# A hybrid attention layer with a written-out instruction order: two loads for two blocks, other engines for the first statistics, other heads in the memory products, and another order

## The chip, the core and the metric

The program runs on one core of a Trainium2 chip. Five engines work side by side, each through its own instructions in order: TensorE (PE; its weight loads are PEld), VectorE (DVE), ScalarE (ACT), GpSimd (POOL) and SyncE (SP), which here only issues transfers. They wait for each other through semaphores. Matrix products land in PSUM, which this kernel uses as 8 banks of 128 x 512 floats. The metric is the device time of one execution in microseconds; lower is better.

## What is computed

The input x has 2048 tokens of width 640. Two residual blocks follow each other:

```
h  = x + A(layernorm(x))           # attention with a memory, 32 heads of 20
h2 = h + silu(layernorm(h) @ w1) @ w2     # 640 -> 1728 -> 640
```

A cuts the tokens into four segments of 512. In each segment and head it forms

```
a_dot = softmax(q k^T * scale + causal mask) v
a_mem = phi(q) M / (phi(q) z + 1e-6)       # phi(t) = t + 1 if t > 0 else exp(t)
o     = g * a_mem + (1 - g) * a_dot        # g = sigmoid(beta), one per head
M    += phi(k)^T v ;  z += sum phi(k)      # for the segments that follow
```

and the four segments' o go through wo. Segment 0 has an empty memory.

## The kernel before

**Layout.** Tokens are handled in 16 blocks of 128, four to a segment. The 32 heads are packed for the array in groups of 128 rows: four heads to a group, 32 rows to a head, of which 20 are used. Heads 0 to 19 fill five groups; the 12 spare rows below the heads of the first three groups, and those of the last two, hold the dimensions of heads 20 to 31, which three further groups (QKV) get by small copies (`vt`). So a segment has eight groups, called ticks here and numbered 0 to 31 over the four segments.

**Tasks.** The work is cut into named tasks, each of which emits the instructions of one step on one engine. The names that the text uses, s a segment, b a block, k a tick:

- `x0, x1, x2, x4, x8, x12`: loads of x. `w_*`: loads of weights. `re_wq0..4`, `re_wk0..4`: copies that rearrange the columns of wq and wk into the packed layout; chunk 0 comes in two halves (`re_wq0`, `re_wq0h`). They can run on ACT, DVE or POOL.
- `n1_st`, `n1_rs`, `n1_ap`, `n1_tp`, `n1_te`, `n1_tr` (b): first layer norm of a block: statistics; one over the root, on POOL; normalization, on DVE; transposes, on PE with an evacuation `te` for blocks 0 to 3, by DMA (`tr`) for the others. `n2_*` is the second layer norm.
- `pr` (segment, group, 0 for q and 1 for k): projections; `qe` evacuates them from PSUM. `ex`, `pa`, `pb`: phi, an exp on ACT and two steps on DVE. `v`, `ve`: the same for v.
- `qk k a|b|e`: scores of a tick, on PE, into four banks; `e k a|b|e`: their exp on ACT, in two instructions of 128 x 1024, or in one of 128 x 2048 where the list says `/W`; `mk`: causal masks on POOL; `av`: products with v; `oe`: their evacuation; `td`, `tm`: transposes back and products with the memory; `nm`: division, on DVE; `ad`: the sum of both parts, on POOL. The e scores serve two ticks.
- `kt`, `mz`, `ma`, `mb`: update of the memory. `ot`, `wo`, `rs`: output projection and first residual. `h1`, `th`, `s`: first matrix of the second block, and silu by a tanh on ACT and a step on DVE. `h2`, `o`, `out`: second matrix, second residual and store.

**Order.** No planner runs when the kernel is built: the whole order of 1432 entries is written out as one list, `ORDER`. Each entry names a task, the engine if there is a choice (`/A` ACT, `/D` DVE, `/G` POOL, `/C` column-tiled products on PE, four 32-column products in place of one), and the buffers it takes (`qk4a0:4,6` takes the PSUM banks 4, 5 and 6, 7). `schedule` replays it, and each engine's program is the list restricted to that engine. A tracker sets the semaphore waits. So an engine never overtakes: an entry that waits holds up all that follow it on its engine, and a bank is given to a new task only behind the task that empties it.

**PE's modes.** PE's products come in three forms: whole array (projections, h1, h2), 32-column tiles (`av`, `mz`, `/C` entries) and 32-row tiles (`qk`). `fill25` and `fill5` are products with zeros ahead of the first real work.

The layer norm's tasks are made in `layer_norm` (L734 on), the memory update in `declare_memory` (L1092 on), the loads in `build` (L584 on).

## Time and profile before

| | |
|---|---|
| median of 3 runs | 296.02 us (295.38 to 296.52) |
| the profiled execution | 295.39 us |
| its span, first to last instruction | 293.7 us |
| TensorE clock granted, mean | 0.999 |
| busy share: PE, DVE, ACT, POOL | 97%, 74%, 74%, 50% |
| instructions: PE, DVE, ACT, POOL | 3786, 450, 258, 294 |

Around the span lie 1.7 us of the time. Instruction durations in the groups include the pipeline's depth, so neighbours on an engine overlap by some 0.1 us; where instructions follow each other without a gap, the time of the merged row divided by their number is the better cost of one. Line numbers (L965) are those of the kernel before.

### The profile page before, as it was taken

Reading aid. Unit: us, or ns where it says so; the run is one execution under the profiler, and the core shown is the slowest. Engines: PE = TensorE matmul, PEld = TensorE weight load, DVE = VectorE, ACT = ScalarE, POOL = GpSimd, SP = SyncE. Lnnn points to the kernel's source line nnn. Section 1 sums busy time; section 2 is a strip of 40 time slices with the busy share of each in tenths; the row PEclk is TensorE's granted clock in tenths of the full one; section 3 lists DMA queues with packets and bytes.
Section 4 is the critical chain, followed back from the end, with each engine's and each line's share of the span. In section 5 each row is a group of like instructions: output and inputs, shape, how many; then the busy total and the mean of one; then the engine's idle time right before and its main releaser. Section 6 shows DMA issues by size and latency. Waiting matters only on the chain.

```text
span 293.7 us, 8932 instructions
## 1 busy us (share of the span) xinstructions
PE 284.1 (97%) x3786; PEld 158.3 (54%) x3786; DVE 217.8 (74%) x450; ACT 216.8 (74%) x258; POOL 147.9 (50%) x294
## 2 busy tenths in 40 slices
...
GB/s 218 336 74 189 144 47 215 122 77 69 113 133 85 141 2 2 148 106 63 92 73 82 46 78 69 35 2 42 90 21 2 2 37 122 77 104 0 0 2 112
DMA packets 48599, 24.75 MB, mean 84 GB/s; under 512 B 38896, under 2 KB 47472, under 8 KB 48560
## 3 DMA queue, kind: packets, MB, share of 16 engines
...
q14 instruction: 9, 0.07, 0.1%
...
## 4 chain that ended last, share of the span: by engine, by line
PE 83%; ACT 8%; DVE 4%; POOL 2%; issue 1%; DMA 1%; ACTq 0%; DVEq 0%
PE ps_all L551 56%; PE ps_all L552 13%; PE ps_all L944 7%; ACT PT L965 6%; PE ps_all L1000 5%; ACT PT L961 1%; POOL rst L767 1%; PE ps_all L1118 1%; DVE stt L755 1%; PE ps_all L1204 1%; DMA x_tok<-in_A_x_dram 1%; DVE xn_rot L773 1%; POOL PT L977 0%; DVE oTs L1016 0%; POOL rst L765 0%
## 5 line engine op out<-in xcount | busy, mean ns | idle before, releaser
L977 POOL TENSOR_SCALAR_AFFINE_SELECT PT<-PT 128x512 bf16<-128x512 bf16 x128 | 83.1, 656 | 51.4 <-ACT PT L965 33.3
L965 ACT ACTIVATE PT<-ps_all 128x1024 bf16<-128x1024 f32 x100 | 96.5, 1038 | 9.2 <-PE ps_all L944 7.5
L961 ACT ACTIVATE PT<-ps_all 128x2048 bf16<-128x2048 f32 x30 | 56.4, 1880 | 7.9 <-PE ps_all L944 7.3
L551 PE MATMUL ps_all<-w_sb,sT 128*128 128x320 bf16 x420 | 61.1, 299 | 0.2
L1217 ACT ACTIVATE th<-ps_all 128x512 f32<-128x512 f32 (+1 forms) x56 | 31.6, 585 | 36.3 <-PE ps_all L551 29.6
L1223 DVE SCALAR_TENSOR_TENSOR sT<-th,ps_all 128x512 bf16<-128x512 f32 (+1 forms) x56 | 36.0, 662 | 24.5 <-ACT th L1217 24.4
L551 PE MATMUL ps_all<-tT,w_sb 128*128 128x512 bf16 x211 | 50.7, 380 | 0.0
L551 PEld LDWEIGHTS ps_all<-w_sb,sT 128*128 128x128 bf16 x420 | 40.1, 98 | 18.0 <-issue 1.6
L551 PEld LDWEIGHTS ps_all<-tT,w_sb 128*128 128x128 bf16 x211 | 19.1, 98 | 22.1 <-issue 1.6
L1078 POOL TENSOR_TENSOR otok<-on 128x320 bf16<-128x320 bf16 x24 | 19.2, 800 | 18.6 <-DVE on L1070 14.6
L755 DVE BATCH_NORM_STATS2 stt<-x_tok 128x6 f32<-128x320 bf16 x60 | 26.2, 479 | 2.3 <-DMA x_tok<-in_A_x_dram 2.0
L1260 DVE SCALAR_TENSOR_TENSOR x_tok<-ps_all,x_tok 128x640 bf16<-128x640 f32 (+1 forms) x17 | 13.2, 782 | 17.3 <-PE ps_all L551 16.6
L765 POOL TENSOR_TENSOR rst<-mvt,eps_c 128x1 f32<-128x1 f32 x32 | 6.6, 206 | 32.1 <-DVE mvt L758 32.0
L868 DVE CAST QK<-ps_all 128x512 bf16<-128x512 f32 x25 | 17.1, 685 | 5.8 <-PE ps_all L551 3.4
L1070 DVE TENSOR_TENSOR on<-ps_all,rd 128x640 bf16<-128x640 f32 x24 | 19.8, 824 | 0.8
L1016 DVE TENSOR_SCALAR oTs<-ps_all,lsc 128x512 bf16<-128x512 f32 x25 | 18.4, 741 | 1.4 <-PE ps_all L1000 1.4
L767 POOL TENSOR_TENSOR rst<-rst,eps_c 128x1 f32<-128x1 f32 x32 | 18.1, 566 | 2.5
L773 DVE TENSOR_SCALAR xn_rot<-x_tok,mvt,rst 128x640 bf16<-128x640 bf16 x32 | 16.5, 519 | 3.6 <-POOL rst L767 2.3
L551 PE MATMUL ps_all<-tT,wkr 128*128 128x512 bf16 (+1 forms) x76 | 18.8, 372 | 0.1
L551 PE MATMUL ps_all<-tT,wqr 128*128 128x512 bf16 (+1 forms) x72 | 18.2, 369 | 0.2
L1000 PE MATMUL ps_all<-PT,Vx 128*32 128x512 bf16 (+3 forms) x384 | 17.0, 301 | 0.1
L551 PE MATMUL ps_all<-wv_sb,tT 128*128 128x320 bf16 x100 | 15.6, 299 | 0.5 <-ACT PT L965 0.4
...
## 6 DMA issues: line engine op xcount, KB each, us to landing
...
x_tok<-in_A_x_dram SPq DMA_DIRECT2D x3, 640.0 KB, 4.6
...
w_sb<-in_B_w_dram SPq DMA_DIRECT2D x1, 640.0 KB, 4.6
```

Source lines behind the costliest of these rows:

```text
L551: return [lambda e: e.matmul(out, lhsT=lhsT, rhs=rhs, start=start, stop=stop)]
L552: return [lambda e, p=p: e.matmul(out[p:p + 32, :], lhsT=lhsT[:, p:p + 32], rhs=rhs, start=start, stop=stop, tile_position=(0, p)) for p i ...
L755: T.add(DV, lambda e, hh=hh: e.bn_stats(out=stt[:, s, 6 * hh:6 * hh + 6], in_=xb[:, 320 * hh:320 * hh + 320]), reads=R((xa, xsub)), writes ...
L767: T.add(PO, lambda e: e.tensor_tensor(out=rst[:, s, :], in0=rst[:, s, :], in1=eps_c[:, 1:2], op=ALU.pow), reads=R((st, ["r"]), (C, ["half" ...
L944: fns.append(lambda e, j=j, o=o, r=r, q0=q0, q1=q1, qa=qa, ka=ka: e.matmul(ps_all[:, o:o + q1 - q0], lhsT=ka[32 * r:32 * r + DH, 128 * j:1 ...
L961: T.add(AC, lambda e: e.activation(out=o, in_=src, func=ACT.Exp, scale=SCALE), reads=[("ps", z.slot + q) for z in (a, b) for q in range(2) ...
L965: T.add(AC, lambda e: e.activation(out=pt[:, pta.slot, q0:q0 + 2, 0:width], in_=sc3[:, b0:b0 + 2, 0:width], func=ACT.Exp, scale=SCALE), re ...
L977: fns.append(lambda e, v=v: e.affine_select(out=v, in_=v, pattern=[[0, 4], [1, 128]], compare_op=ALU.is_ge, fill=0.0, base=0, channel_mult ...
L1000: fns.append(lambda e, j=j, r=r, h=h, pa=pa, pt=pt, co=co, q0=q0, ji=ji: e.matmul(bank(po)[32 * r:32 * r + 32, q0:hi], lhsT=vtile(vx)[:, j ...
L1070: T.add(DV, lambda e: e.tensor_tensor(out=on[:, ona.slot, :, :].rearrange("p b (x e) -> p b x e", e=DH), in0=v[:, :, :, 0:DH], in1=r2.unsq ...
L1217: T.add(AC, lambda e: e.activation(out=th[:, tha.slot, lo:hi], in_=bank(ps)[:, lo:hi], func=ACT.Tanh, scale=0.5), reads=R((ps, [0])), writ ...
L1223: T.add(DV, lambda e: e.scalar_tensor_tensor(out=sT[:, f, lo:hi], in0=th[:, tha.slot, lo:hi], scalar=1.0, in1=bank(ps)[:, lo:hi], op0=ALU. ...
```

## The change

Five things change together.

1. Blocks 2 and 3 of x come by two loads of 160 KB, not by one of 320 KB.
2. Statistics of blocks 0, 1 and 3 are made on DVE, that of block 2 on ACT; before, blocks 1 and 2 were on ACT. On ACT the mean is now scaled in its own instruction (`n1_mn2`), off the way to the variance.
3. For blocks 0, 1 and 3 the small constant under the root is added on DVE at the end of the statistics, so that POOL makes the root with one instruction (pow) in place of two (add, pow).
4. In the memory update the second head of the first three groups is 20 heads on, not 16: the layout puts head 20 + 4c + r below head 4c + r. The products keep their number and size; with stride 16 the rows of phi(k) of one head met the values of another.
5. `ORDER` is another list of 1433 entries. Nearly every entry changes place, and some change engine: on POOL there are 8 `re` entries in place of 5, on ACT 12 `oe` in place of 7, 6 `ve` in place of 9, and 31 exps `/W` in place of 30. PE has the same 510 tasks in both lists.

The code that changes:

```diff
-    load_x(2, 2, -97, 4.79, "fix", (SP,))
+    load_x(2, 1, -97, 2.4, "fix", (SP,))
+    load_x(3, 1, -96.5, 2.4, "fix", (SP,))
...
-                T.add(AC, lambda e: e.activation(out=o, in_=xb, func=ACT.Identity, scale=1.0 / D, accum_out=mvt[:, s, 0:1]),
-                      reads=R((xa, xsub)), writes=R((st, ["mv"]), (xn, [0])))
-                T.add(AC, lambda e: e.activation(out=stt[:, s, 0:1], in_=mvt[:, s, 0:1], func=ACT.Identity, scale=f),
-                      reads=R((st, ["mv"])), writes=R((st, ["s0", "s1"])))
+                T.add(AC, lambda e: e.activation(out=o, in_=xb, func=ACT.Identity, scale=f / D, accum_out=stt[:, s, 0:1]),
+                      reads=R((xa, xsub)), writes=R((st, ["s0"]), (xn, [0])))
...
+            if early:
+                T.add(DV, lambda e: e.tensor_scalar(out=mvt[:, s, 1:2], in0=mvt[:, s, 1:2], scalar1=EPS, scalar2=None,
+                                                    op0=ALU.add),
+                      reads=R((st, ["mv"])), writes=R((st, ["mv"])))
+        early = tag == "n1_" and b in (0, 1, 3)
+        onact = tag == "n1_" and b == 2
...
+            if early:
+                T.add(PO, lambda e: e.tensor_tensor(out=rst[:, s, :], in0=mvt[:, s, 1:2], in1=eps_c[:, 1:2], op=ALU.pow),
+                      reads=R((st, ["mv"]), (C, ["half"])), writes=R((st, ["r"])))
+                return
...
-                heads = [(4 * c, 16, 2)] if c < 3 else [(12, 8, 3)] if c == 3 else [(16, 8, 2), (28, 1, 1)]
+                heads = [(4 * c, 20, 2)] if c < 3 else [(12, 8, 3)] if c == 3 else [(16, 8, 2), (28, 1, 1)]
```

The start of the list, up to the scores of tick 2, before and after:

```diff
-epsg0:0 halfc epsc zpad warm:0 iota x0:1 n1_st0:3 x1:0 x2:2,3 w_q0:0 w_q1 w_k0 w_k1 w_wv:0 beta sel n1_st1/A:0,3
-fill25:3 n1_rs0 n1_ap0:0 n1_tp0:3 mt3 mta3 fill5:0 n1_st2/A:4,2 n1_st3:1 n1_rs1 n1_ap1 n1_tp1:0 n1_te0/D:1 re_wq0/A:0
-mt0 n1_rs3 n1_ap3:3 n1_tp3:6 n1_te1 n1_rs2 mt2 re_wq0h/G n1_ap2 n1_te3 re_wk0:0 re_wq1/G x4:4,5,6,11 n1_tp2:4 n1_te2
-pr000x.0:0 pr000x.1 qe000x/D:0 re_wk0h re_wq2 pr001x.0:7 pr001y.0:3 pr000y.0:1 pr000y.1/C qe000y/D x8:8,7,10,9
-pr001y.1/C qe001y/D pr001x.1/C qe001x ex001:0 pr010.0/C:4 qk0a0:2,6 e0a2:6 pr010.1 qe010/D:0 re_wk1/G re_wq3 pr011.0:1
-pr011.1 qe011/D zf0 zf1 e0a0 qk0b0:4,6 e0b2/W:5 lsc0 mtb3 re_wk4/G re_wk2 re_wq4 mta0 mtb0 mta2 mtb2 mm10 mzc10 mm9
-mm11 re_wk3/G pa001:2 pb001 pr020.0:0 pr020.1 qe020:0 pr021.0:1 pr021.1 qk0e0:2,4 v01.0/C:6 n1_st4:5 mm8 n1_rs4 vpad2
-mk0a e0e2/W:3 qe021/D vt06:0 n1_st7:1 mk0b n1_rs7 vt03 w_w1_1:0 vt09 n1_ap4:2 n1_tr4:0 kt00:0 vt00 n1_st11:5 w_w1_4
-ex021:0 v00.0/C:0 v00.1 ve00:0 qk1a0:2,4 e1a2:0 e1a0 v01.1/C ve01/D mk1a n1_st6:2 n1_rs6 v02.0/C:0 v02.1/C ve02
-n1_st5:6 n1_rs5 qk1b0:4,6 e1b0/W:4 pr031.0:3 pr031.1 qe031/D:0 ex031:1 n1_ap6:0 v03.0:0 v03.1 ve03 qk2a0:2,6 e2a0:1
...
+mt3:0 mt2 x0:4 x1:8 x2:9 x3:0 zpad warm:0 mt1 iota sel mta2 mt0 vpad0 fill25:2 fill5:0 n1_st2:2,3 n1_mn2 n1_st0:4
+halfc w_q0:0 n1_st1:7 w_q1 w_k0 w_k1 w_wv:0 n1_rs0 mta3 n1_ap0:2 n1_tp0:0 n1_te0:1 n1_st3:0 n1_rs1 n1_ap1:0 n1_tp1:2
+epsc n1_rs2 n1_ap2 n1_tp2:4 n1_rs3 n1_ap3:2 n1_tp3:6 re_wq0/G:0 re_wq1/G mta0 mtb0 n1_te1 pr000x.0/C:3 re_wq0h
+pr000x.1 n1_te2/D n1_te3 qe000x:0 pr000y.0:5 pr000y.1 qe000y re_wk0:0 pr001y.0:0 pr001x.0:7 x4:1,2,10,3 re_wk0h
+pr001y.1 re_wq2/A pr001x.1 qe001x qe001y/D ex001:1 pr010.0:1 qk0a0:4,6 e0a0:6 pr010.1 qe010/D:0 e0a2 pr020.0:2 pr020.1
+qk0b0:4,0 e0b0:3 e0b2 beta w_wo:0 qe020/D:0 pa001:0 pb001 mm4 vpad1 mtb2 re_wk1/G pr011.0/C:3 pr011.1/C epsg0 qe011/D
+ex011:0 re_wk3/G mtb3 mm10 re_wk2/G pr021.0/C:7 pr021.1/C re_wq3/G re_wk4/G vpad2 mm11 mta1 qk0e0:2,4 e0e0/W:2 v00.0:0
+lsc0 v00.1 ve00:0 n1_st4:7 mm2 n1_rs4 re_wq4/G mm0 n1_st7:5 n1_rs7 mk0b qe021/D v01.0:6 kt00:0 w_w1_3:0 n1_ap4:3
+n1_st6:0 vt00:0 n1_tr4:2 x8:5,6,7,11 lsc1 qk1a0:4,2 e1a0/W:0 ex021:1 v01.1 ve01/D mtb1 mm1 v02.0:0 v02.1/C n1_st5:1
+n1_rs5 qk1b0:4,6 ve02/D n1_ap7:0 pr031.0:2 pr031.1 qe031/D:0 zf0 e1b0/W:4 v03.0:0 v03.1 ve03/D pa031:1 n1_rs6 n1_ap6:2
+mm8 ex031:2 pb031 n1_st10:2 qk2a0:3,6 e2a0:1 pr030.0/C:2 pr030.1 n1_ap5:3 lsc2 qe030/D zf1 mm3 mk0a mm6 mk1a e2a2
```

Around the scores of tick 23, before and after:

```diff
-ad19 n1_rs13 h1_1_7_0.1/C th1_7_0:0 s1_7_0 h1_1_8_0.1/C th1_8_0:1 av21:3 oe21:0 h1_1_9_0.0:4 h1_1_9_0.1 th1_9_0:0
-h1_1_10_0.0:7 n1_ap14:2 s1_8_0 v30.0:5 v30.1 ve30:1 s1_9_0 n1_ap13:1 tm21:2 h1_1_10_0.1 td21 th1_10_0:1 nm21:0,1
-qk23a0:5,0 e23a2:2 mk22e s1_10_0 n1_ap15:3 h1_1_11_0.0:4 h1_1_11_0.1 e23a0 mk22a qk23b0:0,2 e23b2/W:1 th1_11_0:1 ad21
...
+th1_4_0:0 s1_4_0 qk22e0:2,4 th1_8_0:1 s1_8_0 mk21b av21:0 e22e2/W:1 h1_1_9_0.0:6 n1_st13:3 n1_st15:2 ad19 n1_rs14
+n1_ap14:2 n1_tr14 n1_rs13 n1_rs15 th1_6_0:1 h1_1_7_0.0:7 h1_1_7_0.1 th1_7_0:0 s1_7_0 n1_ap13:3 n1_tr13 s1_6_0 oe21:1
+h1_1_9_0.1 th1_9_0:0 s1_9_0 tm21/C:2 v30.0/C:4 v30.1/C ve30:0 mk22a h1_1_10_0.0/C:7 h1_1_10_0.1/C th1_10_0:1
+qk23a0:4,0 e23a2:5 mk22b mk22e e23a0 mk23a td21 nm21:1,0 h1_1_11_0.0:6 h1_1_11_0.1 n1_ap15:0 n1_tr15 kt21:4 s1_10_0
+qk23b0:0,2 e23b0/W:3 th1_11_0:1 v32.0/C:4 v32.1/C ve32/D av22:7 oe22/D:0 ex241:0 v31.0/C:0 v31.1/C ve31 mk23b ad21
```

185 lines of the change are left out of this document (94 added, 91 removed).

## The prediction

> **What bounds the kernel now.** I read the page's busy shares first, then the table of stretches, then what PE waited for.
>
> ```profile
> PE 284.1 (97%) x3786; PEld 158.3 (54%) x3786; DVE 217.8 (74%) x450; ACT 216.8 (74%) x258; POOL 147.9 (50%) x294
> ```
>
> PE is busy for 284.1 of 293.7 us, but a busy PE need not be at its peak. The stretches say where it is idle; the first numbers behind the length are the busy times of PE, PEld, DVE, ACT and POOL.
>
> ```profile
> 0.00:10.00 10.00, 7.61 (x53) 5.48 (x54) 5.40 (x15) 8.26 (x17) 5.59 (x24) 1.00 0.81 261
> 10.00:30.00 20.00, 19.98 (x263) 9.96 (x265) 17.67 (x51) 18.03 (x22) 15.81 (x42) 1.00 0.73 177
> 30.00:40.00 10.00, 8.13 (x181) 4.13 (x169) 8.75 (x20) 9.68 (x12) 8.04 (x18) 1.00 0.43 98
> 40.00:50.00 10.00, 8.73 (x137) 3.85 (x138) 8.36 (x20) 9.87 (x13) 7.92 (x20) 1.00 0.60 170
> 50.00:60.00 10.00, 9.75 (x151) 4.39 (x148) 8.33 (x18) 9.86 (x12) 5.84 (x12) 1.00 0.50 105
> 60.00:270.00 210.00, 208.82 (x2883) 117.08 (x2876) 159.59 (x317) 156.30 (x180) 104.66 (x179) 1.00 0.36 67
> ```
>
> So there are three places to gain or lose. Up to 10 us PE has little real work. From 30 to 60 it idles 1.87 + 1.27 + 0.25 = 3.39 us, while ACT is busy 29.41 of 30: this stage runs at ACT's pace. From 60 on it idles 1.18 us in 210. The rest is PE's own work.
>
> **PE's work does not change.** Counted in the two lists, PE has the same 510 tasks with the same columns, and in both 188 of them follow a task of another array form. More entries are column-tiled in some places and fewer in others; the tiles' four products run side by side. The other heads (stride 20 for 16) leave the memory products' count and sizes alone. I take 0 for all of this. The last entries, `h2_13_3_0` to `out13_1`, are the same, so the end behind 291 us stays.
>
> **The front.** The rows of the first ten microseconds (start, length):
>
> ```profile
> 0.80 1.36 SPq L584 DMA_DIRECT2D x_tok<-in_A_x_dram  x3
> 3.09 0.89 DVE L755 BATCH_NORM_STATS2 stt<-x_tok 128x6 f32<-128x320 bf16 x2 [2.02 <-DMA x_tok<-in_A_x_dram]
> 4.01 0.21 DVE L758 BATCH_NORM_AGGREGATE mvt<-stt 128x2 f32<-128x12 f32 x1
> 4.30 0.19 POOL L765 TENSOR_TENSOR rst<-mvt,eps_c 128x1 f32<-128x1 f32 x1 [3.04 <-DVE mvt L758]
> 4.57 0.56 POOL L767 TENSOR_TENSOR rst<-rst,eps_c 128x1 f32<-128x1 f32 x1
> 5.25 0.54 DVE L773 TENSOR_SCALAR xn_rot<-x_tok,mvt,rst 128x640 bf16<-128x640 bf16 x1 [0.94 <-POOL mt L670]
> 7.08 0.82 DVE L792 CAST tT<-ps_all 128x640 bf16<-128x640 f32 x1
> 8.89 0.45 DVE L773 TENSOR_SCALAR xn_rot<-x_tok,mvt,rst 128x640 bf16<-128x640 bf16 x1 [0.51 <-POOL rst L767]
> 9.40 0.45 PE L782 MATMUL ps_all<-ident,xn_rot 128*128 128x128 bf16 x5 [0.51 <-DVE xn_rot L773]
> 9.46 0.85 DVE L714 COPY wkr<-sT 128x240 bf16<-128x240 bf16 x2
> 9.69 0.71 PE L551 MATMUL ps_all<-tT,wqr 128*128 128x256 bf16 x5
> 10.47 0.85 POOL L714 COPY wkr<-sT 128x400 bf16<-128x400 bf16 x2 [0.21 <-DMA sT<-in_A_wk_dram]
> x_tok<-in_A_x_dram SPq DMA_DIRECT2D x3, 640.0 KB, 4.6
> L662 DVE TENSOR_SCALAR zf<-zf 128x32 f32<-128x32 f32 x1 | 0.2, 173 | 0.0
> L657 DVE TENSOR_SCALAR lsc<-lsc 128x8 f32<-128x8 f32 x1 | 0.7, 674 | 0.0
> ```
>
> Now DVE makes three statistics, each 0.89 + 0.21 and the added constant. No row shows that addition; the small ones give 0.17 to 0.67, and I take 0.2, as most small ones are near the lower end. Statistics of block 0 then end at 4.45. The new list puts those of block 1 ahead of the first normalization on DVE: 4.45 + 1.3 = 5.75, and the saved POOL step (0.19 + 0.08) is lost there, since the root is ready at 5.06. Normalization 0 ends at 6.25 (before: 5.79), statistics 3 at 7.55, and normalizations 1, 2, 3 at 0.45 each at 8.9, against 9.34 before. Block 2 is not on this path as long as its statistics on ACT and its two POOL steps (0.19 + 0.56) end before 8.0, when normalization 2 comes up; x2 is issued where the pair was, with half the bytes. So the last transposes end near 9.4 and not 9.85, and the first projection can start at 9.4, not 9.69.
>
> Part of this is given back. DVE then has, in a row, two copies of chunk 0 of wq (some 0.6), an evacuation of 0.82 and the two copies of wk's chunk 0 (0.85): the last end near 11.2, some 0.2 after PE has made the query products that stand before the key products. The extra load pushes the weights' issues by one, 1.36/3 = 0.45; the keys' second part, awaited on POOL until 10.47, is now due near 10.9, before DVE reaches it. `x4` waits for those copies of wk, so it leaves SP near 11.2; it takes 4.6 and is there at 15.8, before its statistics, which stand behind the products of v at some 18 us. The load of wo moves up to the place right behind it on SP, where nothing early follows but transposes of block 4. Sum: -0.2, between -0.6 (all of the earlier start stays) and +0.8 (the addition at 0.67 three times, less the 0.6).
>
> **The stage at ACT's pace.**
>
> ```profile
> 20.17 0.71 ACT L833 ACTIVATE sT<-ps_all 128x640 bf16<-128x640 f32 x1
> 25.52 0.33 PE ps_all L944 x4
> 25.13 0.63 ACT L874 ACTIVATE ex<-w_sb 128x512 bf16<-128x512 bf16 x1
> 26.25 1.93 ACT L965 ACTIVATE PT<-ps_all 128x1024 bf16<-128x1024 f32 x2
> 28.06 1.89 ACT L961 ACTIVATE PT<-ps_all 128x2048 bf16<-128x2048 f32 x1
> 30.79 18.68 ACT L965 ACTIVATE PT<-ps_all 128x1024 bf16<-128x1024 f32 x20 [0.32 <-PE ps_all L944]
> L1014 ACT ACTIVATE oTs<-ps_all,lsc 128x512 bf16<-128x512 f32 x7 | 4.7, 686 | 0.9 <-PE ps_all L1000 0.9
> ```
>
> In a run one half exp costs 18.68/20 = 0.93, so two cost what one `/W` costs (1.89 less its overlap): merging gains nothing. From the first exp of tick 0 to the last of tick 7 the old list has 32 halves, 4 whole ones, 4 `ex`, 3 `ve`, 1 `qe`; the new one 30, 5, 5, 1, 1 and one `oe`. That is +0.63 - 2 x 0.70 + 0.69 = -0.1. Moreover two `ve` and a `qe` of those saved, less an `ex`, lie before the scores of tick 2, where PE and not ACT sets the pace (PE idles 0.02 of 20 us): the new ACT stands idle there, and all it gains is its backlog: the scores of tick 2 are ready at 25.52 + 0.33, and ACT came to them at 26.25, 0.4 later. One idle time of 0.32 at 30.79 may go or stay. Net -0.1 from the list and -0.2, half of the backlog: -0.3. Ends: -1.2 and +0.9. The gain would be PE work drawn into the idle time: ahead of the scores of tick 9 the new list has all memory products and one half projection (3 x 0.24) more, and one of 2 x 0.24 less. The loss would be `oe1` at 0.69 right before the exps of tick 4, whose scores wait for it in turn, and 0.2 of a new idle time.
>
> ```profile
> 183.43 0.93 PE ps_all L1118 x94
> L551 PE MATMUL ps_all<-tT,w_sb 128*128 128x512 bf16 x211 | 50.7, 380 | 0.0
> ```
>
> 0.93 + 0.72 - 0.48 = 1.2 us: the lower end. I take less because at the scores of tick 10 both lists have called the same PE work but for one half of `wo1`, which the new one lacks.
>
> **The one long wait behind 60 us.**
>
> ```profile
> 164.94 0.55 POOL L767 TENSOR_TENSOR rst<-rst,eps_c 128x1 f32<-128x1 f32 x1
> 165.52 0.74 DVE L773 TENSOR_SCALAR xn_rot<-x_tok,mvt,rst 128x640 bf16<-128x640 bf16 x1 [0.27 <-POOL rst L767]
> 166.19 0.18 DVE L1064 TENSOR_TENSOR rd<-ps_all,epsg 128x32 f32<-128x32 f32 x1
> 166.78 0.82 DVE L1070 TENSOR_TENSOR on<-ps_all,rd 128x640 bf16<-128x640 f32 x1
> 167.75 0.40 PE L944 MATMUL ps_all<-QKV 20*128 20x384 bf16 x8 [0.66 <-DVE on L1070]
> ```
>
> Scores 23b need the bank of `nm21`; on DVE `nm21` stands behind `n1_ap13`, which waits for a root that POOL makes only behind masks and an `ad`. In the new list root and normalization come well ahead, but `nm21` itself (166.19 to 167.60, 1.4) now starts when `td21` ends and is covered by four to five products of 0.24 alone, 1.2. What is late next is `nm21`, by some 0.3. I take -0.3, between -0.66 and +0.5 (a bank that comes free later by another step of 0.8). Other waits of the new order can't be read in a trace of the old one: between 0 and +1.2, what 210 us now hold; I take 0, since both lists leave the same 188 changes of form and as much PE work between the scores.
>
> Sum: -0.2 - 0.3 - 0.3 = -0.8. The profiled execution took 295.39, so 294.6; the median of the runs stands 0.63 above it, so 295.2.
>
> **Rivals.**
>
> *Faster by over 0.5%* (what a measurement of this kernel can tell from no change; 1.48 us). The work drawn forward fills PE's idle time: -1.2 there, -0.6 in the front, -0.66 at tick 23: 296.02 - 2.5 = 293.6. For it: PE idle is 3.39 us and the list does call more PE work by tick 9. Against it: scores wait for banks that ACT empties, and ACT's list is as long as before.
>
> *Slower by over 0.5%.* POOL comes too late in the front. It gets `re_wq0`, `re_wk2`, `re_wq3` and `re_wq4` and loses `re_wq0h`.
>
> ```profile
> L714 POOL COPY wkr<-sT 128x400 bf16<-128x400 bf16 x3 | 1.5, 515 | 0.2 <-DMA sT<-in_A_wk_dram 0.2
> L714 POOL COPY wkr<-sT 128x240 bf16<-128x240 bf16 x1 | 0.4, 388 | 0.0
> L881 DVE TENSOR_SCALAR phiK<-w_sb 128x512 bf16<-128x512 bf16 x1 | 0.6, 622 | 0.0
> L881 DVE TENSOR_SCALAR phiQ<-QK 128x512 bf16<-128x512 bf16 x15 | 6.4, 429 | 0.0
> ```
>
> Chunk 2 is 0.52 + 0.39, and the last two chunks have two small copies for the second: 1.2 each; in sum 3.4 us more. POOL idles 4.2 us between 10 and 30, so by the sum it fits, with 0.8 to spare. But `pr021` waits for `re_wk2`: from the last early root near 8.2 POOL has chunks wq0, wq1, wk1, wk3 and some eight constants of 0.2 to 0.3 before it, which makes 15; PE needs it after 29 products of 0.24 or less from 9.4 on, at 16.3 or sooner. From some 1.3 us late on, PE idles as long as POOL is late, exps start late, and nothing behind gives it back; past 2.3 us of it the kernel is over 0.5% slower. All 3.4 us exposed give 295.2 + 3.4 = 298.6.
>
> *DVE slows beside POOL's copies.* A `pa` step beside a copy of POOL took 622 ns, the others 429 on average: 0.19. The new list has 20 such copies for 12; 8 x 0.19 = 1.5 us on DVE, which is busy 17.67 of 20 there. All of it exposed gives 296.7, within 0.5%. The Trainium skill ("SBUF — State Buffer", the single rule on the shared port pair) has it that VectorE and GpSimd hold that pair exclusively for a whole instruction, the other waiting; the two rows here agree in direction, with 0.19 us. By that rule alone each of the eight could hold DVE for a copy's whole length; as an estimate that is 8 x 0.4 = 3.2 us and 298.4.
>
> *The front is not earlier.* Statistics 1 stand ahead of normalization 0, so the first transposes come no sooner, and the additions cost 0.4 each: the front's +0.8, 296.2.
>
> **How the numbers follow.** The forecast 0.33; faster 0.32; DVE beside copies 0.07 and no earlier front 0.07, both within 0.5%; slower 0.21, most of it POOL, some a new wait that I did not see. That gives 0.32, 0.47, 0.21. The forecast's own range is 293.9 (-0.6 - 1.2 - 0.3 = -2.1) to 296.4 (+1.2, the new waits' end). The full range, 292.7 to 297.8, takes in the faster case and slower ones up to 2.6 us of exposed delay.
>
> **What would show it.** Right: the first projection at 9.2 to 9.6 us; PE idle of 2.3 to 3.6 us between 30 and 60 with ACT at 9.6 of 10 or more; no PE wait of over 0.4 us near 165. Wrong: PE idle between 10 and 30 above 0.5 us, which would be POOL or DVE in the front; ACT idle over 1 us in 30 to 60; PE idle behind 60 above 2 us; or PE's busy time itself other than 284.

## The result, and the profile after

Over six executions the changed kernel takes 298.80 us in the median (298.25 to 301.83); the kernel before, beside it, 295.83 (295.13 to 296.52). The ratio is 1.0119, with a 95% interval of 1.0073 to 1.0166. A repetition (told below) gives 298.86 against 295.56, 1.0092 [1.0065, 1.0118]. So the change costs some 3 us, about 1%. The forecast was 295.2, with a range up to 297.8: wrong in sign, and the time lies above the range. The profiled execution took 298.25, its span 296.3, which is 2.6 more than before.

The table of stretches of the changed kernel, with the columns as in the prediction (length; busy PE, PEld, DVE, ACT, POOL; clock; then the DMA engines' share and GB/s):

```profile
0.00:10.00 10.00, 7.43 (x64) 5.16 (x64) 7.32 (x21) 6.51 (x10) 6.41 (x25) 1.00 0.79 246
10.00:30.00 20.00, 19.41 (x195) 9.34 (x193) 16.33 (x37) 18.15 (x23) 16.84 (x52) 1.00 0.84 212
30.00:40.00 10.00, 7.20 (x147) 3.64 (x146) 8.76 (x23) 8.93 (x10) 7.45 (x15) 1.00 0.43 91
40.00:50.00 10.00, 8.52 (x128) 3.14 (x124) 7.25 (x16) 9.89 (x12) 7.26 (x16) 1.00 0.46 104
50.00:60.00 10.00, 9.41 (x181) 4.88 (x177) 9.37 (x21) 9.89 (x12) 6.33 (x14) 1.00 0.62 148
60.00:270.00 210.00, 208.11 (x3055) 116.89 (x3040) 157.19 (x315) 157.59 (x181) 105.38 (x181) 1.00 0.34 66
```

The reader is to see three things. PE idles 0.59 us between 10 and 30 (before 0.02), 4.87 between 30 and 60 (before 3.39) and 1.89 from 60 to 270 (before 1.18). ACT, which should set the pace from 30 on, has 1.07 us idle between 30 and 40 alone, where it had 0.32. And PE's busy time over the whole span is 283.8 against 284.1: its work is the same, so all of the loss is idle time. The waits of PE in the changed kernel (engine, buffer and line; what it waited for; us in total, times, the longest):

```profile
PE ps_all L959 <- ACT PT L976: 1.4, 2, 0.8
PE ps_all L797 <- DVE xn_rot L788: 1.3, 2, 1.1
PE ps_all L959 <- ACT PT L980: 1.2, 4, 0.5
...
PE ps_all L1015 <- DVE w_sb L883: 0.9, 1, 0.9
PE ps_all L551 <- DVE Vx L849: 0.6, 1, 0.6
PE ps_all L959 <- DVE otok L1067: 0.6, 1, 0.6
...
PE ps_all L551 <- DVE tT L807: 0.3, 1, 0.3
...
PE ps_all L551 <- DVE wqr L715: 0.2, 1, 0.2
```

The waits for `PT` are scores that want banks which exps still empty. Those of 0.9 for `w_sb` and of 0.6 for `otok` (a division on DVE, which holds up scores of tick 5) were not there before, and no step of the prediction has them.

Following the same tasks of PE through both traces shows where the 2.7 us arise. Start in the changed kernel less start in the one before:

| task | us |
|---|---|
| first projection `pr000x` | -0.6 |
| scores of tick 0, 1, 2 | +0.1, +0.3, +0.3 |
| scores of tick 3 | +1.4 |
| scores of tick 4 and 7 | +2.0, +2.1 |
| scores of tick 10 (less PE's own work done by then) | +1.6 |
| scores of tick 12 (the same) | +2.3 |
| scores of tick 24, 31, end | +3.0, +2.7, +2.7 |

In the two corrected rows PE's idle time is compared in place of its starts; they are good to some 0.2. So in this execution the front loses 0.3, the stage between 25 and 51 us about 1.8, some 0.5 comes back by tick 10, and 0.7 goes near 82 us. Behind that little more is lost.

**The front.** Rows of the timeline of the changed kernel:

```profile
4.26 0.15 DVE L760 TENSOR_SCALAR mvt<-mvt 128x1 f32<-128x1 f32 x1
4.66 0.74 ACT L747 ACTIVATE xn_rot<-x_tok 128x640 bf16<-128x640 bf16 x1 [1.32 <-DMA x_tok<-in_A_x_dram]
9.05 0.63 DVE L715 COPY wqr<-sT 128x160 bf16<-128x160 bf16 x2 [0.43 <-DMA sT<-in_A_wq_dram]
9.06 0.51 PE L552 MATMUL ps_all<-tT,wqr 128*32 128x256 bf16 x12
...
15.60 1.01 DVE L896 TENSOR_SCALAR phiK<-w_sb 128x512 bf16<-128x512 bf16 x1
```

The added constant costs 0.15, not 0.2, and the first projection starts at 9.06, 0.6 earlier. But its second half waits for weights that land later than before, as the prediction said of the issue order, and an evacuation comes behind the copies of those weights on DVE: 0.2 and 0.3 us in the table of waits. By the first scores nothing is left. By those of tick 1 it is +0.3: the step at 15.60 takes 1.01 beside copies on POOL (the same line takes 0.28 alone, see the run with the masks moved), and the next scores wait 0.26 for the evacuation behind it. The front isn't the same in every execution, though. The repetition of this kernel has +0.3 at tick 2 again. But in seven other profiles of kernels with the same list up to here, or with a few masks moved in it, the scores of tick 2 stand at -0.4 to -0.1, and in three where block 2 lands late at +1.0 to +1.2. So a loss in the front is not shown.

**The stage at ACT's pace.** The timeline from 24 to 32 us, DVE, then POOL, ACT and PE:

```profile
26.60 0.75 DVE L896 TENSOR_SCALAR phiK<-w_sb 128x512 bf16<-128x512 bf16 x1
27.27 0.75 DVE L788 TENSOR_SCALAR xn_rot<-x_tok,mvt,rst 128x640 bf16<-128x640 bf16 x1
27.94 0.88 DVE L902 TENSOR_TENSOR phiK<-phiK,ex 128x512 bf16<-128x512 bf16 x1
28.75 0.89 DVE L754 BATCH_NORM_STATS2 stt<-x_tok 128x6 f32<-128x320 bf16 x2
...
30.20 0.68 DVE L883 CAST w_sb<-ps_all 128x512 bf16<-128x512 f32 x1
...
30.95 0.68 DVE L883 CAST w_sb<-ps_all 128x512 bf16<-128x512 f32 x1
...
26.56 1.98 POOL L992 TENSOR_SCALAR_AFFINE_SELECT PT<-PT 128x512 bf16<-128x512 bf16 x3
...
31.67 0.63 ACT L889 ACTIVATE ex<-w_sb 128x512 bf16<-128x512 bf16 x1 [0.99 <-DVE w_sb L883]
...
37.58 0.72 ACT L1029 ACTIVATE oTs<-ps_all,lsc 128x512 bf16<-128x512 f32 x1
...
28.80 1.24 PE L551 MATMUL ps_all<-tT,wqr 128*128 128x512 bf16 x5
30.93 0.73 PE L1015 MATMUL ps_all<-PT,sT 128*32 128x512 bf16 x16 [0.89 <-DVE w_sb L883]
```

DVE is late here, and both PE and ACT wait for it. PE's `av0` needs the bank that `qe030` empties (the cast at 30.20): 0.89. ACT's `ex041` needs what `qe041` writes (the cast at 30.95): 0.99, in a stage in which ACT's time is the stage's time. On DVE the statistics of block 10 (28.75) stand ahead of both, and ahead of those three steps lie that take 0.75, 0.75 and 0.88 beside POOL's masks. The load of blocks 8 to 11 (`x8`) lands at 28.72 in this trace, so the statistics could not have started sooner in any case. At 37.58 stands `oe1` on ACT, right before the exps of tick 4, as the prediction said it would.

**Near 82 us and near 170 us.**

```profile
79.63 1.46 DVE L788 TENSOR_SCALAR xn_rot<-x_tok,mvt,rst 128x640 bf16<-128x640 bf16 x2
81.02 0.85 DVE L902 TENSOR_TENSOR phiQ<-phiQ,ex 128x512 bf16<-128x512 bf16 x1
81.79 0.81 DVE L849 CAST Vx<-ps_all 128x640 bf16<-128x640 f32 x1
82.66 0.32 PE L551 MATMUL ps_all<-Mzb,phiQ 128*128 128x84 bf16 x4 [0.56 <-DVE Vx L849]
168.65 0.19 DVE L1079 TENSOR_TENSOR rd<-ps_all,epsg 128x32 f32<-128x32 f32 x1 [0.81 <-PE ps_all L551]
...
169.26 0.82 DVE L1085 TENSOR_TENSOR on<-ps_all,rd 128x640 bf16<-128x640 f32 x1
168.44 1.25 PE L551 MATMUL ps_all<-tT,w_sb 128*128 128x512 bf16 x5
170.23 0.40 PE L959 MATMUL ps_all<-QKV 20*128 20x384 bf16 x8 [0.54 <-DVE on L1085]
```

`tm8` takes the bank that `ve23` empties, and `ve23` stands on DVE behind a queue without gaps whose steps are long again. The wait at tick 23, which was to go, is still there: 0.54 in place of 0.66.

### The profile page after: what moved, and what is told of

The parts are those of the page before. It is cut to its first block, busy times and chain, and to the rows that moved or that the text cites. A ratio compares the mean times of both kernels' runs of the same rounds, so it can differ in the third digit from the quotient of the medians.

```text
span 296.3 us, 9115 instructions
## 1 busy us (share of the span) xinstructions
PE 283.8 (96%) x3873; PEld 157.6 (53%) x3873; DVE 216.5 (73%) x445; ACT 216.9 (73%) x255; POOL 149.7 (51%) x299
## 4 chain that ended last, share of the span: by engine, by line
PE 76%; DVE 11%; ACT 8%; DMA 2%; issue 1%; SPq 1%; DVEq 0%; ACTq 0%
PE ps_all L551 52%; PE ps_all L552 11%; PE ps_all L959 7%; ACT PT L980 6%; PE ps_all L1015 4%; DMA sT<-in_A_wq_dram 2%; DVE xn_rot L788 2%; ACT PT L976 1%; DVE phiQ L902 1%; DVE stt L754 1%; PE ps_all L1133 1%; DVE oTs L1031 1%; DVE on L1085 1%; PE ps_all L1219 1%; DVE x_tok L1197 1%
## 5 line engine op out<-in xcount | busy, mean ns | idle before, releaser
L980 ACT ACTIVATE PT<-ps_all 128x1024 bf16<-128x1024 f32 x98 | 94.3, 1025 | 12.3 <-PE ps_all L959 10.7
L976 ACT ACTIVATE PT<-ps_all 128x2048 bf16<-128x2048 f32 x31 | 58.3, 1880 | 3.8 <-PE ps_all L959 3.3
L551 PE MATMUL ps_all<-w_sb,sT 128*128 128x320 bf16 x374 | 53.8, 299 | 0.0
L551 PE MATMUL ps_all<-tT,w_sb 128*128 128x512 bf16 x202 | 46.9, 379 | 0.0
L551 PEld LDWEIGHTS ps_all<-w_sb,sT 128*128 128x128 bf16 x374 | 35.6, 98 | 15.3 <-issue 1.5
L551 PE MATMUL ps_all<-tT,wqr 128*128 128x512 bf16 (+1 forms) x82 | 20.3, 371 | 0.7 <-DVE tT L807 0.3
L780 POOL TENSOR_TENSOR rst<-mvt,eps_c 128x1 f32<-128x1 f32 x29 | 6.2, 215 | 27.2 <-DVE mvt L757 27.1
L551 PE MATMUL ps_all<-wo_sb,tT 128*128 128x320 bf16 x120 | 17.9, 299 | 0.0
L782 POOL TENSOR_TENSOR rst<-rst,eps_c 128x1 f32<-128x1 f32 x29 | 16.4, 567 | 2.3
L1031 DVE TENSOR_SCALAR oTs<-ps_all,lsc 128x512 bf16<-128x512 f32 x20 | 14.8, 745 | 3.4 <-PE ps_all L1015 3.3
L551 PE MATMUL ps_all<-wv_sb,tT 128*128 128x320 bf16 x110 | 17.0, 299 | 0.4 <-ACT PT L980 0.2
```

Source lines behind the costliest of these rows:

```text
L551: return [lambda e: e.matmul(out, lhsT=lhsT, rhs=rhs, start=start, stop=stop)]
L976: T.add(AC, lambda e: e.activation(out=o, in_=src, func=ACT.Exp, scale=SCALE), reads=[("ps", z.slot + q) for z in (a, b) for q in range(2) ...
L980: T.add(AC, lambda e: e.activation(out=pt[:, pta.slot, q0:q0 + 2, 0:width], in_=sc3[:, b0:b0 + 2, 0:width], func=ACT.Exp, scale=SCALE), re ...
```

## The experiments

All ratios are to the kernel before, run beside. The kernel before and the two built on its code (the old list with the new one behind it, and the old list with `nm21` moved) keep its head stride of 16 in the memory update; all others have 20. "The end" is the start of PE's last product in the profiled execution less that of the kernel before (the changed kernel: +2.7); these come from one execution each, so the ratio stands beside them. A part of each end is the front, which varies, so the shift of PE's scores is also given from tick 2 to tick 7, which is the stage alone:

| kernel | at tick 2 | from tick 2 to 7 | from 7 to the end |
|---|---|---|---|
| changed | +0.3 | +1.8 | +0.5 |
| the same, repeated | +0.3 | +1.7 | +0.5 |
| DVE's order | -0.2 | +1.1 | +0.8 |
| with `oe1` on DVE too | -0.1 | +0.8 | +0.3 |
| all mends | +1.1 | +0.8 | +0.2 |

The expectations name theories by letters; those on which the readings rest are: A, DVE is late near 30 us, and `oe1` on ACT costs its length; F and M, the bank layout of the scores of ticks 3 and 4; G, POOL's masks lengthen DVE's steps; J, the late load `x8`; N, the granted clock.

### The code alone

The four edits of the code (loads, statistics, root, heads) with the list of before:

```diff
-x2:2,3
+x2:2 x3:3
-n1_st1/A:0,3
+n1_st1:0
-n1_st2/A:4,2
+n1_st2:4,2 n1_mn2
-n1_ap1
+n1_ap1:1
```

> The old list with all four changes of the code (x2 and x3 in two loads, statistics of block 3 on VectorE, the constant added on VectorE and one GpSimd step per root, stride 20 in the memory products) and none of the new order. Theory A (the loss of the changed kernel comes from the new order; its pieces: 1.1 us where DVE reaches two evacuations late near 30 us, 0.6 us for oe1 on ACT near 38 us, 0.7 us of a wait near 83 us): the parts cost nothing that lasts, ratio to the kernel before 0.997 to 1.003. Rival B (the added DVE steps and the extra load cost, and the order only shows it): 1.004 or more, with the shift in place before the scores of tick 1.

Measured: 295.97, 1.0026 [0.9998, 1.0054]. The four parts cost nothing that can be told from no change, so the new list holds most of the loss. In this trace the first scores come 0.6 later and the end 0.4; the old front itself comes out 0.1 and 0.4 later in two other kernels that have it unchanged.

### Half of the list

One kernel has the old list up to the scores of tick 9 and the new one behind; the other the new one up to the exps of tick 9 and the old one behind.

> The kernel before, its list up to the scores qk9a0 (near 60 us), then what is left in the order of the new list (with some other buffers, 14 of them). In the traces PE's start times less its own work stand 1.9 us later in the changed kernel at that place and 2.7 us at the end. Theory A: the first 1.9 is absent and 0.8 stays, most of it the wait at 83 us: +0.8 us, ratio 1.003. Rival C (what is lost early is regained by other idle time, and the loss is made behind 60 us): +2.7 us, ratio 1.009.

Measured: 313.39, 1.0604 [1.057, 1.0639]. This settles nothing: the joint itself broke the order. Wait table of this kernel:

```profile
PE ps_all L552 <- DVE QK L868: 13.0, 1, 13.0
```

Transfers that the joint put behind each other on SP held steps of DVE, and PE stood 13 us at that one place.

> The changed kernel, its list up to the exp e9a0 (near 63 us), then what is left in the order of the old list (9 buffers differ). Theory A: +1.9 us, ratio to the kernel before 1.006. Rival C: 0 to +0.5 us, ratio 1.000 to 1.002.

Measured: 300.46, 1.0168 [1.0122, 1.0215]. Here too the joint has a wait of its own (1.7 us near 68 us), and ahead of it the memory products wait 0.9 near 60 us, which the changed kernel's profile doesn't have; so the ratio is no measure. But up to tick 7 the first 60 us show the same loss as the changed kernel (scores of tick 2 at -0.4, of tick 7 at +1.5), and behind the joint the old order adds nothing (+3.9, then +3.7 at the end). Most of the loss arises in the first 60 us, as far as this run can say. That a part of it lies behind 60 us it doesn't exclude.

### DVE's order near 30 us

`qe030` right behind its product, statistics 10 behind `ve10`, and its root on POOL next to that of block 8:

```diff
-pb031 n1_st10:2 qk2a0:3,6 e2a0:1 pr030.0/C:2 pr030.1 n1_ap5:3 lsc2 qe030/D
+pb031 qk2a0:3,6 e2a0:1 pr030.0/C:2 pr030.1 qe030/D n1_ap5:3 lsc2
...
+v10.1/C ve10/D:0 n1_st10:2
```

> The changed kernel with three entries moved: on DVE the evacuation qe030 comes directly behind its projection, ahead of normalization n1_ap5, and the statistics n1_st10 (1.1 us, not needed before 40 us) behind ve10; on POOL the root n1_rs10 behind the masks that follow it. Theory A: av0's wait for the bank of qe030 (0.94 us of PE) and ex041's wait for qe041 (0.99 us of ACT idle) were one delay of DVE and both fall below 0.3; -1.0 us against the changed kernel, 297.8 us, ratio to the kernel before 1.007 to 1.009. Rival D (ACT's pace and its own list set the stage anyway, and the wait moves to the next exps): no change, ratio 1.011 to 1.013.

Measured: 297.88, 1.0086 [1.0058, 1.0113]; the end at +1.7, which is 1.0 less, though half of that is its front. In the stage it loses 1.1 where the changed kernel loses 1.8 and 1.7. The timeline of ACT in this kernel:

```profile
29.56 0.60 ACT L882 ACTIVATE w_sb<-ps_all 128x512 bf16<-128x512 f32 x1
30.05 0.62 ACT L889 ACTIVATE ex<-w_sb 128x512 bf16<-128x512 bf16 x1
```

`ex041` follows without a gap, and `av0` waits for nothing. By the ratios alone this step isn't told from the changed kernel (the intervals overlap); the trace shows both waits gone, as A had it, and 0.7 us gained in the stage. The expected 1.0 was met by the help of the front.

### `oe1` on DVE

The kernel above, with `oe1` on DVE ahead of statistics 11, and statistics 9 later:

```diff
-td0/C:1 nm0:1,0 oe1:0 v11.0:2
+td0/C:1 nm0:1,0 v11.0:2
...
-e3b0/W:0 epsg1 n1_st11:5
+e3b0/W:0 epsg1 oe1/D:0 n1_st11:5
```

> The kernel of the run with VectorE's order mended (ratio 1.0086 to the kernel before), and oe1 made on VectorE as in the old list, in the place of the statistics n1_st9, which go behind pb011. In its trace oe1 takes 0.65 us of ACT (35.95 to 36.60) right ahead of the exps of tick 4, in the stage where ACT is busy 9.5 to 9.9 of 10. Theory A (what ACT gets added there is added to the time): -0.6 us, ratio 1.006 to 1.007. Rival E (PE, which idles at the same place, or VectorE, which has to make oe1 now, holds the stage as long): within 0.2 us, ratio 1.008 to 1.009.

Measured: 296.90, 1.0029 [0.9993, 1.0065]; the end at +1.0, another 0.7 less. Of that the stage holds 0.3; the rest lies behind 85 us, at places where kernels with the same list there differ as much. The interval lies below that of the changed kernel, and touches that of its repetition. ACT now has fourteen exps in a row where `oe1` stood:

```profile
36.70 13.32 ACT L980 ACTIVATE PT<-ps_all 128x1024 bf16<-128x1024 f32 x14 [0.50 <-PE ps_all L959]
```

So two of the steps in which the list differs, DVE's order near 30 and `oe1`, hold 1.0 of the stage's 1.8 us by the traces. By the medians they are worth more together (298.80 and 298.86 against 296.90).

### The merged exp of tick 3

The DVE order of above, with `e3b0/W` as two instructions of 128 x 1024:

> The kernel of the run with VectorE's order mended (ratio 1.0086), with the merged exp e3b0/W split into e3b0 and e3b2. Theory F (a merged exp costs ACT nothing but holds all four banks until its end; the scores of tick 4, which need two of them, come 0.88 us late on PE, and ACT then idles 0.45 us at 39 us): PE's wait there shrinks to 0.2 or less, ACT's idle time goes, -0.4 us, ratio 1.007. Rival (merging is free, as the prediction had it): no change, 1.008 to 1.009.

Measured: 298.25, 1.0053 [1.0016, 1.009], and in the trace the scores of tick 4 wait for a bank as before, 0.91 us, the end at +1.8. F falls: those scores take all four banks of `qk3b0`, and the second half exp ends when the merged one did. The ratio's apparent gain isn't supported by the trace of its profiled execution, and the two intervals overlap. That merging gains or costs nothing was in the prediction.

### Why DVE is late: masks, and a load

First the masks and constants of POOL are moved away from the three long steps (`mk0a`, `mk0e` earlier, `mk1a` and four constants later); DVE's list stays.

> The changed kernel with GpSimd's masks mk0a and mk0e ahead of two roots (they run near 23 to 25 us, beside statistics and evacuations of VectorE), and mk1a and some small copies behind the root n1_rs10 (after 30 us), so that no mask runs from 26.5 to 28.5 us; VectorE's order is that of the changed kernel. Theory G (pa031, n1_ap6 and pb031 took 0.75, 0.75 and 0.88 us there because a mask of GpSimd ran beside them, elsewhere 0.43 to 0.44; these 1.1 us are what made qe030 and qe041 late): the three take 0.43 to 0.5 each, av0's wait of 0.94 us falls below 0.3, -0.9 us, ratio 1.008 to 1.010. Rival (their length has another cause, such as the place of the data): they stay at 0.75 or more, ratio 1.011 to 1.013.

Measured: 299.21, 1.0099 [1.0062, 1.0137]. DVE's and ACT's timeline:

```profile
25.89 0.28 DVE L896 TENSOR_SCALAR phiK<-w_sb 128x512 bf16<-128x512 bf16 x1
26.30 0.45 DVE L788 TENSOR_SCALAR xn_rot<-x_tok,mvt,rst 128x640 bf16<-128x640 bf16 x1
26.66 0.42 DVE L902 TENSOR_TENSOR phiK<-phiK,ex 128x512 bf16<-128x512 bf16 x1
27.82 0.89 DVE L754 BATCH_NORM_STATS2 stt<-x_tok 128x6 f32<-128x320 bf16 x2 [0.74 <-DMA x_tok<-in_A_x_dram]
...
31.21 0.63 ACT L889 ACTIVATE ex<-w_sb 128x512 bf16<-128x512 bf16 x1 [1.25 <-DVE w_sb L883]
```

The steps fall from 0.75, 0.75 and 0.88 to 0.28, 0.45 and 0.42, 1.2 us in sum: G's mechanism is there. The time does not fall, since statistics 10 now wait for their data. `x8`, the load of blocks 8 to 11, is issued late. SP's timeline of the kernel before, then of the changed one:

```profile
10.35 0.92 SPq L584 DMA_DIRECT2D x_tok<-in_A_x_dram  x2
```

```profile
22.52 1.11 SPq L584 DMA_DIRECT2D x_tok<-in_A_x_dram  x1
```

Before, `x4` and `x8` went out together near 10.4; now `x8` goes at 22.5, behind six other transfers, and lands at 27.8 in the run above. So the same kernel again with `x8` right behind `x4`:

```diff
-pr001x.0:7 x4:1,2,10,3 re_wk0h
+pr001x.0:7 x4:1,2,10,3 x8:5,6,7,11 re_wk0h
```

> The changed kernel with the masks moved as before (ratio 1.0099), and the load x8 called directly behind x4, as early as in the old list; VectorE's order is still the changed kernel's. In the trace without masks beside them pa031, n1_ap6 and pb031 took 0.28, 0.45 and 0.42 us, yet n1_st10 then stood 0.74 us for x8 to land (27.82 us), so qe030 was late all the same. Theory J (two causes one behind the other: VectorE slowed by the masks, and x8 issued late; only without both is qe030 in time): n1_st10 no longer waits, av0's wait (0.72 us) and ACT's idle time ahead of ex041 (1.25 us) fall below 0.4, -0.8 us, ratio 1.006 to 1.008. Rival (the earlier load of 640 KB delays x4 and the weights, or something else holds qe030): ratio 1.009 or more.

Measured: 297.85, 1.0057 [1.0026, 1.0088]. Two rows of its timeline:

```profile
28.63 0.88 DVE L754 BATCH_NORM_STATS2 stt<-x_tok 128x6 f32<-128x320 bf16 x2
...
32.02 0.63 ACT L889 ACTIVATE ex<-w_sb 128x512 bf16<-128x512 bf16 x1 [0.43 <-DVE w_sb L883]
```

The statistics follow the step before them without a wait, `av0` doesn't wait, and ACT's gap is 0.43 for 1.25 (J had below 0.4). From the scores of tick 2 to those of tick 4 this kernel loses 1.1, the one above 1.9; behind that its profiled execution is spoilt by a stretch at half clock (told at the end). So two causes lie one behind the other: take the masks away, and the load still holds DVE; with both gone the gap nearly closes. That is J, and the same place that the reordering of DVE's list mended in another way. What the early load does with the masks left in place was not run. By the ratios this kernel isn't told from the changed one's repetition.

### `ve23`, and everything together

In the changed kernel `ve23` goes to ACT (`ve23/D` to `ve23`).

> The changed kernel with one edit: the evacuation ve23 on ACT, as in the old list, not on VectorE. In the changed kernel tm8 waited 0.72 us at 82.66 for the banks that ve23 gives back, behind a backlog of VectorE that lasts from 72 us on. Theory A: that wait goes, and nothing near it takes its place; -0.7 us, ratio 1.009 to 1.010. Rival H (the next product of PE waits for the same backlog of VectorE or for ACT's exps instead): within 0.2 us, ratio 1.011 to 1.013.

Measured: 299.37, 1.0092 [1.0052, 1.0131]. In the trace `tm8`'s wait is gone, and between the scores of tick 10 and 12 this kernel's shift grows by 0.65 us where the changed one's grows by 1.2 in both its profiles. So the wait costs some 0.6 in the trace; the ratios are too wide to show it. The end, at +4.3, shows none of it: block 2 came late (tick 2 at +1.0), and the memory products near 62 us waited 0.7 in this execution.

Then all of these mends in one kernel: DVE's order, `oe1`, `ve23`, `x8`, and `td21 nm21` ahead of the scores of tick 23.

> The changed kernel with all edits that bear on the new order's losses: VectorE's order mended and oe1 on VectorE (together 1.0029), ve23 on ACT, x8 early, and td21 and nm21 called ahead of the scores qk23a0, so that the bank for qk23b0 is free in time. Theory A, by the pieces: ve23 -0.5 us, td21 -0.4 us, x8 nothing more: -0.9 us against 1.0029, ratio 0.999 to 1.001. Rival (the remaining loss lies in the sum of small waits that no single edit reaches): 1.002 to 1.003.

Measured: 296.73, 1.0028 [1.001, 1.0047], no better than with the first two alone. Its profiled execution also shows a thing that no list sets:

```profile
5.66 0.74 ACT L747 ACTIVATE xn_rot<-x_tok 128x640 bf16<-128x640 bf16 x1 [2.31 <-DMA x_tok<-in_A_x_dram]
```

The same load of block 2, issued in the same place, is there at 5.66 and not at 4.66 as in the changed kernel, and the first scores come 1.1 later. So the mends may have gained more than this execution shows; that stays open. From tick 2 to 7 this kernel still loses 0.8, as the one with two mends. Not the loss but the waits can be named: in every version of the new order up to here PE's scores wait 0.84 to 0.91 for the last exp of tick 3 (tick 4), 0.5 to 0.7 and 0.55 (tick 5) and 0.55 (tick 7). The old order has other waits in their place, so what each costs on balance isn't shown.

### The old list with the new parts that should be good

The old list with `nm21` ahead of the normalization of block 13, so that the wait at tick 23 goes:

```diff
-n1_ap13:1 tm21:2 h1_1_10_0.1 td21 th1_10_0:1 nm21:0,1
+tm21:2 h1_1_10_0.1 td21 th1_10_0:1 nm21:0,1 n1_ap13:1
```

> The kernel before with one entry moved: the normalization n1_ap13 behind nm21 on VectorE. It tests the prediction's step on the long wait at 167.75 us by itself: nm21 can start when td21 ends and qk23b0's wait of 0.66 us falls to 0.3 or less by the prediction; -0.3 to -0.6 us, ratio 0.998 to 0.999. Rival (another step takes the wait over, as the new list still has 0.5 us there): ratio 1.000, wait of 0.5 us or more.

Measured: 298.57, 1.0073 [1.0044, 1.0102]: slower. The wait at the scores is gone, and in its place, in the wait table:

```profile
PE ps_all L552 <- DMA tT<-xn_rot: 1.6, 1, 1.6
```

The normalization now comes later, so the transposed block arrives late at the products of v. What the prediction gained at tick 23 is held by whichever of the two steps comes second.

The second takes the new front up to the first exp with `x8` early, and the old list behind it, with the edit above.

> The changed kernel's code and its list up to the exp e0a2 (with x8 called behind x4), then the old list, with n1_ap13 behind nm21. Theory A (the front is the part of the new list that gains, 0.2 to 0.4 us, and the old order is the better one behind it): -0.2 for the front and -0.4 for nm21, ratio 0.997 to 0.999. Rival (the new front leaves VectorE, GpSimd or SyncE later than the old list behind it expects): 1.001 or more.

Measured: 298.80, 1.007 [1.0042, 1.0098].

```profile
17.81 0.23 ACT L661 ACTIVATE zf<-beta_bc 128x32 f32<-128x32 bf16 x1 [2.69 <-DMA beta_bc<-in_A_beta_dram]
...
18.08 0.18 DVE L663 TENSOR_SCALAR zf<-zf 128x32 f32<-128x32 f32 x1 [1.64 <-ACT zf L661]
...
18.64 1.25 PE L551 MATMUL ps_all<-tT,wkr 128*128 128x512 bf16 x5 [1.41 <-DVE wkr L715]
```

`pr021` waits 1.41 for its rearranged weights, whose copy stands on DVE behind the constant `zf1`. That one waits for `zf0` on ACT, and `zf0` for the load of beta, which this list issues at 11.38 (before: 4.87). So the joint made this wait by a late load; it is not the prediction's rival, whose copies are late on POOL. A second wait, of 1.6 us near 88 us, makes most of the rest.

### One load or two

The changed kernel once more, and beside it the changed kernel with blocks 2 and 3 in one load again (`x2:9,0` for `x2:9 x3:0`).

> The changed kernel itself once more, beside the three others. In the traces so far of kernels with the new front, block 2's statistics on ACT begin with the landing of x2, at 4.26 to 4.87 us seven times and at 5.57 to 5.82 us three times; in the late case the first scores come 1.2 us later. Expected: ratio 1.010 to 1.014, and its spread of more than 2 us over the runs again.

> The changed kernel with x2 and x3 in one load of 320 KB again. In the old front the pair landed at 5.5 to 5.9 us. Theory K (the two loads gain when x2 lands early, and the new order behind them needs it early): statistics on ACT begin at 5.5 us or later each time, the first scores come some 1 us later than in the changed kernel's profile, ratio 0.5 to 1 us above that of the changed kernel beside it (1.013 to 1.016). Rival L (the second load delays the weights, and that costs as much as it gains): the same as the changed kernel within 0.3 us.

Measured: 298.86, 1.0092 [1.0065, 1.0118], and 299.18, 1.0117 [1.0084, 1.015]. With one load the statistics of block 2 start at 5.28 us on ACT and the first scores come 0.7 later than before; with two they start at 4.04 in the repetition (first scores +0.35) and 4.66 in the first profile (+0.1), but at 5.66 in another (+1.2). So the split brings them forward in most executions; of that 0.3 us are left in the medians, less than these runs can tell.

### The banks of ticks 3 and 4, and the clock

The remaining waits of 30 to 60 us are scores that wait for banks. Here the list of `oe1` is given another layout: tick 3's exp split, `qk4a0` in other banks, and the products of v between the scores:

```diff
-qk3b0:6,4 e3b0/W:0
+qk3b0:6,4 e3b0:0 e3b2
...
-v11.0:2 qk4a0:4,6
+qk4a0:2,6 v11.0:4
...
-av2:1 v11.1 oe2/D:1 e4a2:2 ve11/D e4a0 qk4b0:0,6 e4b0:4
+e4a2:2 qk4b0:0,6 v11.1 ve11/D e4a0 e4b0:4 vt02 vt07 qk4e0:0,2 av2:4 oe2/D:1
```

> The kernel with VectorE's order mended and oe1 on VectorE (1.0029), with other banks at ticks 3 and 4: the new list gives the scores qk4a the very four banks of qk3b, so PE waits 0.88 us for the last exp of these, and ACT then idles 0.50 us (36.70 us). Here e3b is split, qk4a takes banks 2, 3, 6, 7, which come free one exp earlier, and v11, qk4b and qk4e are reordered to suit. Theory M (that is what is left of the stage's loss): ACT's idle time at 36 us falls below 0.15, -0.5 us, ratio 1.001. Rival (the wait moves to qk4b or qk4e, since PE has other work to do in between): 1.003.

Measured: 301.10, 1.0177 [1.0146, 1.0209]. M falls: PE waits 1.07, 0.61, 0.59, 0.62 and 1.38 us between 34 and 47 us, where the kernel that it starts from waits 0.84, 0.56 and 0.55. The clock in the stretches of this kernel:

```profile
34.50:36.50 2.00, 0.44 (x5) 0.18 (x6) 1.93 (x7) 2.00 (x3) 0.26 (x2) 0.92 0.22 40
36.20:39.60 3.40, 3.15 (x18) 1.29 (x18) 0.42 (x1) 3.00 (x5) 3.00 (x8) 0.50 0.25 52
```

PE has 0.44 us of work in two, and then runs at half the clock for 3.4 us. The same layout on top of all mends:

> The kernel with all edits (1.0028), with the same other banks at ticks 3 and 4. Theory M: -0.5 us, ratio 1.001 and, where x2 lands early, below the kernel before. Rival: 1.003.

Measured: 300.23, 1.014 [1.0104, 1.0177], with the clock at half from 36.5 to 46.7. Whether the clock costs the time can be asked directly: products with zeros (`fill8`, twice `fill5`) put into PE's idle time of the first of these two kernels, `fill8:3` ahead of `qk4a0:2,6`, `fill5:0` ahead of `v11.0:4` and of `qk4b0:0,6`.

> The kernel with other banks at ticks 3 and 4 (ratio 1.0177, granted clock 0.982 to 0.994 in all six runs), with 18 products with zeros of 256 columns (fill8 and twice fill5, 0.1 us each) put into PE's three idle times from 34.4 to 37.3 us. In that kernel's trace PE has 0.39 us of work in the 2.1 us from 34.4 on, and from 36.4 to 39.8 the granted clock is 0.50; the same drop follows such a stretch in three other traces. Theory N (too little work on PE for some 2 to 4 us halves its clock, and that costs 1.7 us or more each time): mean clock 1.0 in at least half of the runs, and the time falls by 1.5 to 2.5 us, ratio 1.009 to 1.013. Rival (the clock falls for a reason outside of PE's own work): clock 0.994 or less again in all runs, ratio 1.016 or more.

Measured: 301.61, 1.0192 [1.0167, 1.0216]. One stretch and one row of PE's timeline:

```profile
46.00:48.00 2.00, 1.68 (x14) 0.72 (x15) 1.97 (x5) 1.18 (x2) 1.04 (x2) 0.50 0.37 41
```

```profile
46.10 0.62 PE L959 MATMUL ps_all<-QKV 20*128 20x384 bf16 x8 [1.38 <-DVE otok L1067]
```

N's half on the clock holds: the drop at 36 us is gone, three of the four executions have a mean clock of 1.00 (of the six without the fill none had), and the one drop left in the profile follows a wait of 1.38 us for DVE. N's half on the time falls: it is no lower, and the three executions at full clock took 301.05 to 302.05. So getting rid of the drop doesn't bring the time back here. That the drop itself costs nothing is not shown: the 18 products with zeros take some 0.1 us each, and part of them may stand in the way. The direct waits are the likelier cause of this layout's loss.

## Why the prediction was wrong, point by point

- **PE's work, 0**: right. 283.8 against 284.1 us, and the code with the old list, the other heads included, isn't told from before (1.0026 [0.9998, 1.0054]).
- **The front, -0.2 (ends -0.6 and +0.8)**: the earlier start was right and larger (9.06 for the forecast 9.4), the additions cheaper (0.15 for 0.2), and the later weights were named. In the first profile the net was too good by 0.3 to 0.5: at the first scores it is +0.1, by tick 2 +0.3. In seven other profiles with nearly the same front it is -0.4 to -0.1 at tick 2, about as forecast. "Block 2 not on this path" held here (4.66 us) but not in every run (5.66 in one), where it costs 1.1.
- **The stage at ACT's pace, -0.3 (ends -1.2 and +0.9)**: this is the step that failed. It came out at some +1.8. Two things are in it. The `oe1` "right before the exps of tick 4" was seen and priced at 0.69; removing it brings 0.3 in the stage of one trace and takes 1.0 off the medians. But it was put at the end of the range, and in the sum ACT's list was only counted, which balances to -0.1. A step of ACT in the middle of its stage is not paid back by steps saved ahead of it, where ACT isn't the bound; the prediction wrote that very argument for the `ve` steps and then drew half of the backlog as a gain. The larger of the two, 0.7, is DVE, for which the stage had no term at all: it reaches `qe030` and `qe041` late, and PE (0.89) and ACT (0.99) wait. The other 0.8 stays open.
- **What was not followed: `x8`.** The prediction traced `x4` and the load of wo through SP and left out `x8`, which the diff shows moved from a place before the first keys' products to one behind the transposes of block 4. It leaves 12 us later; statistics 10, ahead of `qe030` and `qe041` on DVE, then can't start before it lands, at 28.72 in the first profile (27.8 in the run without the masks), and with the masks in place that limit and DVE's own lateness coincide (28.75).
- **Rival "DVE slows beside POOL's copies"** (296.7): its mechanism was right and its place and price wrong. The price, 0.19, came from a mean that has lengthened steps in it; against 0.28, what such a step takes alone, the row of 622 ns is 0.34 longer. In the front one step shows it (1.01 at 15.60), which costs 0.2 in the first profile and nothing in the others, where it takes 0.37 to 0.55. What matters is three steps at 27 us beside masks, 0.47, 0.30 and 0.46 longer (0.75, 0.75, 0.88 less 0.28, 0.45, 0.42), on the one path where PE and ACT wait for DVE.
- **Rival "POOL comes too late in the front"** (up to 298.6): not in the changed kernel, where no PE product waits for `wkr`. The 1.4 us with the new front before the old list are a wait for copies too, but on DVE and for another reason. That 298.6 lies near the result is chance.
- **The wait near 167 us, -0.3**: it came to about -0.1. "Late next is `nm21`" was right. It takes 1.43 us (168.65 to 170.08), but the five products that cover it start 0.2 before it, and the scores 0.15 behind its end: 0.54 in place of the forecast 0.3.
- **Other new waits, 0 (ends 0 and +1.2)**: 0.6 at `tm8`, within the ends, and gone with `ve23` on ACT. The term was put at nothing because both lists have as many changes of form and as much PE work between the scores, which says nothing of a backlog on DVE.
- **Its own signs**: PE idle of 4.87 us between 30 and 60 (2.3 to 3.6 forecast), ACT idle of 1.3 there (over 1 was to mean wrong), PE idle of 0.59 between 10 and 30 (over 0.5) and the wait of 0.54 near 170 (none over 0.4 forecast) all spoke against it; the first projection at 9.06 was sooner than its 9.2 to 9.6; PE idle behind 60 stayed under 2.

For the profiled execution the causes that the runs support are 0.7 and 0.3 in the stage and some 0.6 at `tm8`, 1.6 of 2.7 us. The front's 0.3 varies between executions, 0.8 of the stage stays unexplained, 0.5 comes back before tick 10, and some 0.5 is spread behind that. The sizes stem from single traces; by ratios only the sum of the stage's two parts is clear (1.0029, and 1.0028 with all mends, against 1.0119 and 1.0092).
